# Strassen's form for slices 8 to 15 of the first MLP, and two kinds of sums moved into PSUM

## The chip, the cores and the metric

The kernel runs on one core of one Trainium2 chip. The metric is the device time of one execution in microseconds (us); lower is better.

## What is computed

A decayed linear attention (2 batches, 8 heads, 768 positions, 64 features a head) gives 1536 tokens of 512 features. Two MLPs follow, each with a hidden width of 2048:

```
h = x @ w_in                      # 1536x512 @ 512x2048
g = h * clip(h + 3, 0, 6) / 6     # second MLP: max(0.01 h, h)
x = g @ w_out                     # 1536x2048 @ 2048x512
```

The weights arrive as 64-bit floats and are turned into 32-bit ones on the chip.

## The kernel before, in words

**Tiles.** The tokens are three tiles t of 512. The hidden width is 16 slices f of 128. A step (l, t, f) is one slice of layer l for one token tile: `gemm1` (lines 465 to 477) makes the hidden block of 128 x 512 in one PSUM bank, an activation follows, and `gemm2` (508 to 525) adds the slice's share to four output banks acc0 to acc3, one for each quarter e of 128 output columns. Every operand is held as a high and a low part (`wh`, `wl`, `xh`, `xl`, `Gh`, `Gl`), and each product of two of them is three matmuls (high x high, high x low, low x high). So `gemm1` is 4 x 3 = 12 matmuls of 128x128 by 128x512, and `gemm2` is 12 as well, three for each e.

**Blocks.** The slices of layer 0 go in blocks of 1, 3, 4, 4, 4, those of layer 1 in four blocks of 4 (`BLOCKS`, line 30). In a block, all slices of a token tile add up in PSUM; then `collect` (527 to 535) adds the four banks to `SUM[t]` in SBUF, on VectorE (line 532), or copies them there in a layer's first block, on ScalarE (line 534). In layer 0, tile 1 uses two "a" banks in place of acc0 and acc1 (`acc_bank`, 505).

**Layer 0.** A step is: `gemm1` into an "h" bank; `gate_a` on ScalarE (line 482), `gate_b` on VectorE (486), `g_high` on ScalarE (492), `g_low` on VectorE (499); `gemm2`.

**Layer 1.** Token tiles 0 and 1 (`PAIR`) and two neighbouring slices form a 2 x 2 block product, which `product` (588 to 605) computes in Strassen's form (Winograd's variant): seven products of 6 matmuls each, four sums of weight halves (`w_sum`, `s_high`, `s_low`, 418 to 437) and four sums of input halves (T1 to T4: `x_sum`, `x_split`, 576 to 586). Products 0, 3, 5, 6 add up in one "h" bank, 1 and 4 in a second one, and 2 in an "a" bank. Between them, `keep` (607, ScalarE, line 610) copies the bank as it stands into an SBUF tile `ux`, and `join` (613, VectorE, line 614) adds a bank to such a copy: these are the blocks C11 (products 0 and 2), C12 and C22; the fourth block is the bank itself after product 6. Tile 2 goes by plain `gemm1` into "a" banks. Between the layers, VectorE and ScalarE split the new inputs and make T1 to T4 (lines 541 to 543 and 577 to 585).

**Weights.** Each half slice is loaded (line 371) and converted by two operations of ScalarE (378, 382) and four of VectorE (388 to 401), then split by one of each (409, 413). There are 6 buffers for a slice's weights ("w"), 4 for raw loads, 3 for conversions ("cv").

**Order.** Nothing is left to a scheduler at run time. `Order.issue` (58 to 112) plays the work through with the costs and buffers given in `add`, and always starts, on an idle engine, the ready operation that is due first; that order is each engine's program. Due times run back from the matmuls: 5.45 us a step in layer 0 (`T_STEP`), a written-out list per block in layer 1 (lines 650 to 665). Buffers are counted as `takes` and `frees`. The pools s, Gx and ux open once the attention is done (`open_late`, 561).

Of the kernel before, what the change touches and what calls it, by code (L numbers as in the profile page):

```python
# [23 lines left out]
P = 128  # L24
# [5 lines left out]
BLOCKS = ((1, 3, 4, 4, 4), (4, 4, 4, 4))  # L30

# [84 lines left out]
def decay_attention_two_mlps(ctx: ExitStack, tc: tile.TileContext, qkk, vv, lam, w1, w2, out):  # L116
# [24 lines left out]
    NS = len(steps)  # L141
    step_of = {}
# [275 lines left out]
    def w_sum(p, i):  # L418
        def fn(_):
            t1, t2, raw = (x.bitcast(F32) for x in (CV[1, 2 * p, 0][0], CV[1, 2 * p + 1, 0][0], RAW[1, 2 * p + 1, 0]))  # L420
# [4 lines left out]
            nc.vector.tensor_tensor(out=out[:, i], in0=a, in1=b, op=op)  # L425
            SB[p, "f"] = out
        return fn

    def s_high(p):
        def fn(_):  # L430
            SB[p] = new("s", [P, 2, 4, 2 * P], F32R)
            nc.scalar.copy(out=SB[p][:, 0], in_=SB[p, "f"])
        return fn

    def s_low(p):
        return lambda _: nc.vector.tensor_tensor(out=SB[p][:, 1], in0=SB[p, "f"], in1=SB[p][:, 0].bitcast(F32),
                                                 op=ALU.subtract)

    alloc_w, composed, low = {}, {}, {}
    for l in range(2):  # L440
        for f in range(NF):
            for j in range(2):
                h = (l, f, j)
                held = l == 1 and j == 0
# [9 lines left out]
            if l and f % 2:  # L454
                p, i = f // 2, None
                for n in range(4):
                    i = add(("dve", 0.43), w_sum(p, n), after=[composed[l, f - 1, 0], composed[l, f, 0], i])
                hi = add(("act", 1.05), s_high(p), after=[i], takes=["s"])
                s_ready[p] = add(("dve", 1.22), s_low(p), after=[hi], frees=["raw"])
                add(("none", 0.0), nothing, after=[i, low[l, f - 1, 0], low[l, f, 0]], frees=["cv"] * 2)  # L460
# [4 lines left out]
    def gemm1(s):  # L465
        def fn(_):
# [3 lines left out]
            ps = PH[s] = new("a" if l else "h", [P, TT], F32)  # L470
# [7 lines left out]

    def gate_a(s):
        def fn(_):  # L480
            U[s] = new("u", [P, TT], F32)
            nc.scalar.activation(out=U[s], in_=PH[s], func=AF.Relu, bias=three, scale=1.0)  # L482
        return fn

    def gate_b(s):
        return lambda _: nc.vector.scalar_tensor_tensor(out=U[s], in0=U[s], scalar=6.0, in1=PH[s], op0=ALU.min,  # L486
                                                        op1=ALU.mult)

    def g_high(s):
        def fn(_):  # L490
            G[s] = [new("G", [P, TT], F32R, n) for n in ("Gh", "Gl")]
# [13 lines left out]
    def acc_bank(s, e):  # L505
        return "a" if e < 2 and steps[s][2] % 2 and not steps[s][0] else f"acc{e}"

    def gemm2(s, e):
        def fn(_):
# [4 lines left out]
            if first:  # L514
# [7 lines left out]
            for n, (a, x) in enumerate(terms):  # L522
                nc.tensor.matmul(ACC[e], a, x, start=(first and n == 0), stop=(last and n == 2))  # L523
# [33 lines left out]
    XT, CS = {}, {}  # L557
# [71 lines left out]
    gates = {}  # L629

    def second(s, gl, w_frees):
# [4 lines left out]
        for e in range(4):  # L636
            bank = acc_bank(s, e)
            prev2 = add(("pe", 0.68), gemm2(s, e), due2[s], after=[gl, w_ready[l, f, 1], prev2],
                        takes=[bank] if first else [], frees=([] if e < 3 else w_frees))
            if not last:  # L640
                continue
            c = add(("dve", 0.69) if b else ("act", 0.58), collect(s, e), due2[s] + T_COLLECT,
                    after=[prev2, *taken.get((t, e), [])], frees=[bank])
            sums.append(c)
            taken[t, e] = [c]
# [3 lines left out]

    n0 = NS // 2  # L650
    at = T_FIRST + T_STEP * n0
    due_p = {}
    for b in range(len(BLOCKS[1])):
        fs = [f for f in range(starts[1][b], starts[1][b + 1])]
        one, two = (lambda i: ("1", fs[i])), (lambda t, i: ("2", b, t, fs[i]))
        before = [("2", b - 1, 2, fs[i] - 4) for i in (2, 3)] if b else []
        for item in [("S", fs[0] // 2), *before, ("S", fs[2] // 2), two(0, 0), two(0, 1), one(0), two(0, 2), two(0, 3),
                     one(1), two(1, 0), two(1, 1), one(2), two(1, 2), two(1, 3), one(3), two(2, 0), two(2, 1)]:
            due_p[item] = at
            at += 9.52 if item[0] == "S" else 2.72  # L660
    b = len(BLOCKS[1]) - 1
    due_p["2", b, 2, NF - 2], due_p["2", b, 2, NF - 1] = at, at + 2.72
    for s in range(n0, NS):
        l, b, t, f = steps[s]
        due1[s], due2[s] = due_p["1", f], due_p["2", b, t, f]

    for s in range(n0):
        l, b, t, f = steps[s]
        last = f + 1 == starts[l][b + 1]
        xs = [x_ready[c] for c in range(t * SPT, (t + 1) * SPT)]  # L670
        g1 = add(("pe", 2.73), gemm1(s), due1[s], after=[w_ready[l, f, 0], prev1] + xs, takes=["h", "G"])
        prev1 = g1
        ua = add(("act", 0.69), gate_a(s), after=[g1], takes=["u"])
        gb = add(("dve", 0.69), gate_b(s), after=[ua], frees=["h"])
        gh = add(("act", 0.63), g_high(s), after=[gb])
        gl = add(("dve", 0.69), g_low(s), after=[gh], frees=["u"])
        sums = second(s, gl, ["G"] + ["w"] * (t == NTT - 1))
        if last and b + 1 == len(BLOCKS[l]):
            sums_of[t], last1[t] = sums, g1
    add(("none", 0.0), open_late, after=att_ops, frees=[n for n in late for _ in range(late[n])])  # L680

    split = {}
    for e in (0, 2):
        hi = add(("act", 1.05), split_x(2, e, False), after=[last1[2]] + sums_of[2][e:e + 2])
        split[2, e] = add(("dve", 1.22), split_x(2, e, True), after=[hi])
        taken[2, e] = taken[2, e + 1] = [split[2, e]]
    x_op = {}

    def split_ops(n, after):
        hi = add(("act", 1.05), x_split(n, False), after=after)  # L690
        x_op[n] = add(("dve", 1.22), x_split(n, True), after=[hi])

    sa, sb = sums_of[PAIR[0]], sums_of[PAIR[1]]
    la, lb = last1[PAIR[0]], last1[PAIR[1]]
    split_ops("B11", [la, *sa[:2]])
    split_ops("B21", [la, *sa[2:]])
    split_ops("B22", [lb, *sb[2:]])
    t1 = add(("dve", 1.22), x_sum("T1", "B12", "B11"), after=[x_op["B11"], *sb[:2]])
    split_ops("T1", [t1])
    t3 = add(("dve", 1.22), x_sum("T3", "B22", "B12"), after=[t1, *sb[2:]])  # L700
    t2 = add(("dve", 1.22), x_sum("T2", "B22", "T1"), after=[t3, x_op["B22"]])
    split_ops("T2", [t2])
    split_ops("T3", [t3, lb])
    t4 = add(("dve", 1.22), x_sum("T4", "B21", "T2"), after=[t2, x_op["B21"]])
    split_ops("T4", [t4])
    for t, e, ops in ((0, 0, [x_op["T1"], t2]), (0, 2, [x_op["T4"]]), (1, 0, [x_op["T3"]]), (1, 2, [x_op["T2"], t4])):
        taken[PAIR[t], e] = taken[PAIR[t], e + 1] = ops

    gate = {}
    for p in range(NF // 2):  # L710
        f1, f2 = 2 * p, 2 * p + 1
        d = due_p["S", p]
        s_at = {(f, t): next(s for s in range(n0, NS) if steps[s][2:] == (t, f)) for f in (f1, f2) for t in PAIR}
        ops = []

        def prod(i, after=(), takes=()):
            an, bn = A_B[i]
            w = s_ready[p] if an[0] == "S" else w_ready[1, 2 * p + int(an[1]) - 1, 0]
            ops.append(add(("pe", 1.36), product(p, i), d + 1.36 * i, after=[w, x_op[bn], *ops[-1:], *after],
                           takes=list(takes)))  # L720
            return ops[-1]

        k1 = add(("act", 0.59), keep(p, 0), after=[prod(0, takes=["h"])], takes=["ux"])
# [71 lines left out]
```

## Time and profile before

| | us |
|---|---|
| three runs | 573.12, 575.12, 575.61 (median 575.12) |
| the profiled execution | 573.51 |
| its span, first to last instruction | 571.3 |
| mean granted TensorE clock in it | 0.995 |

In the profile, PE is TensorE, PEld its weight loads (they overlap matmuls), DVE VectorE, ACT ScalarE, POOL GpSimd. A name as `h<-xh,wh` is output and inputs; L475 is line 475. "Idle before" is the engine's idle time just before an instruction, with what ended it. A matmul's recorded duration (389 ns) includes its way through the array, and the next one starts before it ends: what one costs is the distance between starts.

### The profile page before, as it was taken

How to read it: one execution, taken by the hardware profiler on the slowest of the kernel's cores; microseconds unless marked ns; L12 is line 12 of the kernel's file. 1: busy time of each engine (PE TensorE's matmuls, PEld its weight loads, DVE VectorE, ACT ScalarE, POOL GpSimd, SP SyncE). 2: the span in 40 equal slices, each digit the busy share in tenths (PEclk: the TensorE clock that was granted, in tenths of full speed). 3: DMA queues.
4: the chain of work that ended last, by engine and by line, in shares of the span. 5: the costliest groups of instructions: out<-in, count | busy, mean ns of one | idle time of the engine just before them, and what ended most of it. 6: DMA issues, size and time to landing. Idle time of an engine off the chain costs nothing.

```text
span 571.3 us, 8498 instructions
## 1 busy us (share of the span) xinstructions
PE 557.7 (98%) x3396; PEld 462.1 (81%) x3396; DVE 414.0 (72%) x676; ACT 304.0 (53%) x510; POOL 28.3 (5%) x33
## 2 busy tenths in 40 slices
PE   8888999999999999999999999999999999999996
PEld 5877888888888888888888888888888888888885
DVE  8678889998848972698879898479864987653222
ACT  5687875557227532564536667477435653443110
POOL 6561000000000000000000000000000000000000
PEclk9899999999999999999999999999999999999999
DMA  8892333224303230012120114213221121000332
GB/s 332 325 357 99 111 110 111 97 87 149 110 1 108 77 110 1 17 57 74 75 74 1 37 38 141 81 38 111 73 75 37 38 74 38 0 1 1 75 73 73
DMA packets 14536, 49.81 MB, mean 87 GB/s; under 512 B 1698, under 2 KB 1698, under 8 KB 14498
## 3 DMA queue, kind: packets, MB, share of 16 engines
q1 hardware_dynamic: 14176, 48.77, 25.3%
q8 instruction: 26, 0.43, 0.3%
q10 hardware_dynamic: 322, 0.52, 0.3%
q14 instruction: 12, 0.10, 0.1%
HBM read 46.14 MB, written 3.15 MB: 86 GB/s over the span
## 4 chain that ended last, share of the span: by engine, by line
PE 91%; DVE 0%; issue 0%
PE acc L523 42%; PE h L475 23%; PE h L602 11%; PE a L475 8%; PE a L523 4%; PE a L602 2%; PE h L308 1%; PE a L296 1%; DVE sums L532 0%; PE pair L271 0%
## 5 line engine op out<-in xcount | busy, mean ns | idle before, releaser
L482 ACT ACTIVATE u<-h,three 128x512 f32<-128x512 f32 x48 | 33.1, 690 | 79.8 <-PE h L475 79.4
L475 PE MATMUL h<-xh,wh 128*128 128x512 f32 x192 | 74.9, 390 | 0.0
L475 PE MATMUL h<-xl,wh 128*128 128x512 f32 x192 | 74.7, 389 | 0.0
L475 PE MATMUL h<-xh,wl 128*128 128x512 f32 x192 | 74.7, 389 | 0.0
L532 DVE TENSOR_TENSOR sums<-acc,sums 128x512 f32<-128x512 f32 x76 | 50.7, 688 | 19.8 <-PE acc L523 19.8
L523 PE MATMUL acc<-Gh,wh 128*128 128x512 f32 x160 | 62.3, 390 | 0.0
L523 PE MATMUL acc<-Gh,wl 128*128 128x512 f32 x160 | 62.3, 389 | 0.0
L523 PE MATMUL acc<-Gl,wh 128*128 128x512 f32 x160 | 62.2, 389 | 0.0
L486 DVE SCALAR_TENSOR_TENSOR u<-u,h 128x512 f32<-128x512 f32 x48 | 32.9, 685 | 26.8 <-ACT u L482 26.7
L409 ACT CAST wh<-t 128x512 fp32r<-128x512 f32 x64 | 38.9, 618 | 24.2 <-DVE t L401 14.5
L523 PE MATMUL acc<-wh,Gh 128*128 128x512 f32 x128 | 49.8, 389 | 0.0
L523 PE MATMUL acc<-wl,Gh 128*128 128x512 f32 x128 | 49.8, 389 | 0.0
L523 PE MATMUL acc<-wh,Gl 128*128 128x512 f32 x128 | 49.8, 389 | 0.0
L401 DVE CUSTOM_DVE_ANT_0 t<-t,c 128x1024 uint16<-128x1024 uint16 x64 | 45.0, 703 | 2.2
L413 DVE TENSOR_TENSOR wl<-t,wh 128x512 fp32r<-128x512 f32 x64 | 42.9, 686 | 4.0 <-ACT wh L409 3.8
L399 DVE SCALAR_TENSOR_TENSOR t<-raw,t 128x512 uint32<-128x512 uint32 x64 | 44.7, 698 | 1.3
L378 ACT ACTIVATE c<-raw 128x512 uint32<-128x512 uint32 x64 | 42.6, 668 | 5.6 <-DVE t L401 4.6
L382 ACT ACTIVATE t<-raw 128x512 f32<-128x512 f32 x64 | 42.5, 664 | 5.0 <-DVE wl L413 5.0
L502 DVE TENSOR_TENSOR Gl<-u,Gh 128x512 fp32r<-128x512 f32 x24 | 16.6, 690 | 39.1 <-ACT Gh L619 39.0
L475 PEld LDWEIGHTS h<-xh,wh 128*128 128x128 f32 x192 | 36.0, 188 | 7.5
L475 PEld LDWEIGHTS h<-xl,wh 128*128 128x128 f32 x192 | 36.0, 188 | 7.5
L475 PEld LDWEIGHTS h<-xh,wl 128*128 128x128 f32 x192 | 36.0, 188 | 7.5
(128 smaller groups left out, 1120.6 us busy)
## 6 DMA issues: line engine op xcount, KB each, us to landing
raw<-w SPq DMA_DIRECT2D x64, 512.0 KB, 3.3
sums<-qkk SPq DMA_DIRECT2D x12, 768.0 KB, 6.8
vs<-vv SPq DMA_DIRECT2D x6, 512.0 KB, 5.4
out<-sums SPq DMA_DIRECT2D x20, 128.0 KB, 2.3
out<-sums ACTq DMA_DIRECT2D x4, 128.0 KB, 3.3
lam_sb<-lam ACTq DMA_DIRECT2D x1, 0.0 KB
```

Source lines behind the costliest of these rows:

```text
L378: nc.scalar.activation(out=CV[h][1], in_=RAW[h][:, :, 0], func=AF.Copy, scale=2.0 ** -29)
L382: return lambda _: nc.scalar.activation(out=CV[h][0].bitcast(F32), in_=RAW[h][:, :, 1].bitcast(F32), func=AF.Abs)
L399: nc.vector.scalar_tensor_tensor(out=t, in0=RAW[h][:, :, 1], scalar=0xC0000000, in1=t, op0=ALU.bitwise_and, op1=ALU.bitwise_or)
L401: nc.vector.tensor_tensor(out=t, in0=t, in1=c, op=ALU.add)
L409: nc.scalar.copy(out=cut(*h, 0), in_=CV[h][0].bitcast(F32))
L413: return lambda e: eng[e].tensor_tensor(out=cut(*h, 1), in0=CV[h][0].bitcast(F32), in1=cut(*h, 0).bitcast(F32), op=ALU.subtract)
L475: nc.tensor.matmul(ps, a[:, 0, ws], x[:, k, :], start=(n == 0), stop=(n == 3 * KC - 1))
L482: nc.scalar.activation(out=U[s], in_=PH[s], func=AF.Relu, bias=three, scale=1.0)
L486: return lambda _: nc.vector.scalar_tensor_tensor(out=U[s], in0=U[s], scalar=6.0, in1=PH[s], op0=ALU.min, op1=ALU.mult)
L523: nc.tensor.matmul(ACC[e], a, x, start=(first and n == 0), stop=(last and n == 2))
L532: nc.vector.tensor_tensor(out=acc, in0=ps, in1=acc, op=ALU.add)
L602: nc.tensor.matmul(ps, ws[a][:, k * P:(k + 1) * P], xs[b][:, k], start=(i < 3 and n == 0), stop=(n == 5), skip_group_check=True)
```

## The change

1. **Layer 0, slices 8 to 15** (blocks 3 and 4, `SINGLE = 3`): tiles 0 and 1 go by `product` as in layer 1, tile 2 by plain `gemm1` into "a" banks. The weight sums are made for these slices too. The input halves exist there only as high and low parts, so VectorE first adds the parts of four halves (`x_whole`), makes T1 to T4 by four differences (`x_diff`), and splits them (`x_split`, high on ScalarE, low on VectorE). The whole values lie in the two "s" buffers until they are split.
2. **C11 in PSUM**, in both layers: `keep` of product 0 copies the "h" bank into an "a" bank, and product 2 adds to it there, with no `join`; products 0 and 1 still start banks of their own.
3. **Half of the sums over blocks, in PSUM**: in blocks 3 and 4 of layer 0, for e = 0 and 2, `seed` copies `SUM[t]` into the bank on ScalarE before the first `gemm2`, and `collect` is a copy back on ScalarE. For e = 1 and 3 VectorE adds as before. Tile 1 uses acc0 and acc1 there.
4. The due times of these blocks are written out as layer 1's; in block 4, tiles 0 and 1 come first and tile 2's `gemm1` between their end and its own `gemm2`.

```diff
+SINGLE = 3
+    paired = lambda l, f: l == 1 or f >= starts[0][SINGLE]
...
-            if l and f % 2:
+            if paired(l, f) and f % 2:
...
-            ps = PH[s] = new("a" if l else "h", [P, TT], F32)
+            ps = PH[s] = new("a" if paired(l, f) else "h", [P, TT], F32)
...
+    seeded = lambda s, e: steps[s][0] == 0 and steps[s][1] >= SINGLE and e % 2 == 0
+    def seed(s, e):
+        def fn(_):
+            n = acc_bank(s, e)
+            ps = PA["seed", s, e] = pool["acc"].tile([P, TT], F32, tag=n, name=n)
+            nc.scalar.copy(out=ps, in_=SUM[steps[s][2]][:, e, :])
+        return fn
...
-            if b:
+            if b and not seeded(s, e):
                 nc.vector.tensor_tensor(out=acc, in0=ps, in1=acc, op=ALU.add)
             else:
                 nc.scalar.copy(out=acc, in_=ps)
...
+    def x_whole(n):
+        t, e = {"B11": (0, 0), "B21": (0, 2), "B12": (1, 0), "B22": (1, 2)}[n]
+        def fn(g):
+            if n in ("B11", "B22"):
+                SPARE[n == "B22"] = pool["s"].tile([P, 2, 2, TT], F32, tag="s", name="x_spare")
+            xh, xl = (x[:, e:e + 2].bitcast(F32) for x in X[PAIR[t]])
+            eng[g].tensor_tensor(out=spare(n), in0=xh, in1=xl, op=ALU.add)
+        return fn
+    def x_diff(n, a, b):
+        return lambda e: eng[e].tensor_tensor(out=spare(n), in0=spare(a), in1=spare(b), op=ALU.subtract)
...
-                    nc.tensor.matmul(ps, ws[a][:, k * P:(k + 1) * P], xs[b][:, k], start=(i < 3 and n == 0),
+                    nc.tensor.matmul(ps, ws[a][:, k * P:(k + 1) * P], xs[b][:, k], start=(i < 2 and n == 0),
...
+    def keep(l, p, i):
+        def fn(_):
+            if i:
+                CS[l, p, i] = new("ux", [P, TT], F32)
+            else:
+                CS[l, p, i] = PA["S", l, p, 1] = new("a", [P, TT], F32)
+            nc.scalar.copy(out=CS[l, p, i], in_=PA["S", l, p, BANK[i]])
+        return fn
...
+            if first and in_seed:
+                start = add(("act", 0.6), seed(s, e), after=[*taken[t, e], bank_last[bank]], takes=[bank])
...
+        if end:
+            line = [*(two(t, i) for t in PAIR for i in range(4)), one(0), one(1), two(2, 0), one(2), two(2, 1), one(3),
+                    two(2, 2), two(2, 3)]
+        else:
+            line = [two(0, 0), two(0, 1), one(0), two(0, 2), two(0, 3), one(1), two(1, 0), two(1, 1), one(2),
+                    two(1, 2), two(1, 3), one(3), two(2, 0), two(2, 1)]
+        for item in [pair(0), *rest, pair(2), *line]:
...
+        k1 = add(("act", 0.59), keep(l, p, 0), after=[prod(0, takes=["h"])], takes=["a"])
+        k5 = add(("act", 0.59), keep(l, p, 1), after=[prod(1, takes=["h"])], takes=["ux"])
+        c11 = prod(2, [k1])
...
+            if l == 0:
+                ua = add(("act", 0.69), gate_a(s), after=[c], takes=["u"])
+                gb = add(("dve", 0.69), gate_b(s), after=[ua], frees=[bank or "ux"])
+                gh = add(("act", 0.63), g_high(s, n), after=[gb], takes=[n])
...
+    for n, after in (("T1", [t2]), ("T2", [t4]), ("T4", [t4]), ("T3", [t3, last1[0, PAIR[1]]])):
+        hi = add(("act", 1.05), x_split(n, False, spare), after=after)
+        x_op[0, n] = [add(halves, x_split(n, True, spare), after=[hi])]
```

## Rows read from the trace of the kernel before

**Rows 1.** The page: span, and each engine's busy time, share, instructions.
```profile
span 571.3 us, 8498 instructions
PE 557.7 (98%) x3396; PEld 462.1 (81%) x3396; DVE 414.0 (72%) x676; ACT 304.0 (53%) x510; POOL 28.3 (5%) x33
```

**Rows 2.** What TensorE waited for: total, times, longest.
```profile
PE pair L271 <- issue: 2.9, 2, 2.2
PE a L296 <- issue: 2.8, 1, 2.8
PE a L296 <- POOL kd L261: 1.1, 1, 1.1
```

**Rows 3.** Busy time by stretch: layer 0's blocks, then two blocks of layer 1.
```profile
49.00:114.30 65.30, 65.30 (x427) 54.22 (x424) 57.99 (x101) 47.15 (x83) 0.00 (x0) 1.00 0.31 103
114.30:179.60 65.30, 65.30 (x289) 54.05 (x288) 50.78 (x89) 32.67 (x55) 0.00 (x0) 1.00 0.25 84
179.60:244.90 65.30, 65.30 (x290) 54.06 (x289) 44.70 (x78) 29.24 (x49) 0.00 (x0) 1.00 0.20 65
244.90:310.20 65.30, 65.30 (x290) 54.07 (x289) 55.52 (x88) 34.31 (x51) 0.00 (x0) 1.00 0.17 57
372.50:435.10 62.60, 62.60 (x278) 51.84 (x277) 44.72 (x77) 35.32 (x61) 0.00 (x0) 1.00 0.20 68
```

**Rows 4.** The chain that ended last, around a pair of layer 1: start, us.
```profile
387.40 1.36 PE h L602 x6
388.76 0.68 PE acc L523 x3
389.44 1.36 PE h L602 x6
390.80 1.36 PE a L602 x6
...
404.40 2.72 PE a L475 x12
```

**Rows 5.** VectorE's groups, shapes apart: count, busy us, mean ns, idle before.
```profile
L532 DVE TENSOR_TENSOR sums<-acc,sums 128x512 f32<-128x512 f32 x76 | 50.7, 688 | 19.8 <-PE acc L523 19.8
L486 DVE SCALAR_TENSOR_TENSOR u<-u,h 128x512 f32<-128x512 f32 x48 | 32.9, 685 | 26.8 <-ACT u L482 26.7
L614 DVE TENSOR_TENSOR ux<-h,ux 128x512 f32<-128x512 f32 x16 | 11.0, 690 | 9.0 <-PE h L602 9.0
L436 DVE TENSOR_TENSOR s<-raw,s 128x1024 fp32r<-128x1024 f32 x8 | 9.8, 1219 | 0.1
L425 DVE TENSOR_TENSOR raw<-t 128x256 f32<-128x256 f32 x16 | 6.7, 420 | 0.2
L577 DVE TENSOR_TENSOR sums<-sums 128x1024 f32<-128x1024 f32 x4 | 4.9, 1220 | 0.0
```

**Rows 6.** VectorE's busy time (fourth figure) around the start of block 3.
```profile
145.00:155.00 10.00, 10.00 (x46) 8.28 (x45) 8.82 (x17) 4.27 (x7) 0.00 (x0) 1.00 0.40 138
155.00:165.00 10.00, 10.00 (x46) 8.29 (x45) 2.62 (x4) 2.01 (x3) 0.00 (x0) 1.00 0.05 21
165.00:179.60 14.60, 14.60 (x66) 12.08 (x65) 11.21 (x21) 8.57 (x15) 0.00 (x0) 1.00 0.11 36
179.60:190.00 10.40, 10.40 (x47) 8.63 (x46) 9.31 (x18) 7.01 (x12) 0.00 (x0) 1.00 0.34 109
```

**Rows 7.** ScalarE's groups, shapes apart: count, busy us, mean ns, idle before.
```profile
L482 ACT ACTIVATE u<-h,three 128x512 f32<-128x512 f32 x48 | 33.1, 690 | 79.8 <-PE h L475 79.4
L610 ACT COPY ux<-h 128x512 f32<-128x512 f32 x24 | 14.1, 588 | 17.8 <-PE h L602 17.8
L534 ACT COPY sums<-acc 128x512 f32<-128x512 f32 x22 | 12.7, 589 | 0.8
L432 ACT CAST s<-raw 128x1024 fp32r<-128x1024 f32 x8 | 8.4, 1050 | 2.4 <-DVE raw L425 2.4
```

**Rows 8.** ScalarE in order of time: the copy after product 0, and a cast.
```profile
388.80 0.59 ACT L610 COPY ux<-h 128x512 f32<-128x512 f32 x1 [0.19 <-PE h L602]
...
391.32 1.05 ACT L432 CAST s<-raw 128x1024 fp32r<-128x1024 f32 x1
```

More of the change, by code (lines that the diff above doesn't have):

```diff
@@ L513, in fn @@
             first, last = f == starts[l][b], f + 1 == starts[l][b + 1]
-            if first:
+            if first and seeded(s, e):
+                ACC[e] = PA["seed", s, e]
+            elif first:
                 n = acc_bank(s, e)
@@ L522, in fn @@
             for n, (a, x) in enumerate(terms):
-                nc.tensor.matmul(ACC[e], a, x, start=(first and n == 0), stop=(last and n == 2))
+                nc.tensor.matmul(ACC[e], a, x, start=(first and n == 0 and not seeded(s, e)), stop=(last and n == 2),
+                                 skip_group_check=seeded(s, e))
             PA["acc", s, e] = ACC[e]
@@ L629, in decay_attention_two_mlps @@
     gates = {}
+    bank_last = {}
     def second(s, gl, w_frees):
@@ L648, in second @@
         return sums
[L650 to L658, printed above, removed]
+    n1, n0 = starts[0][SINGLE] * NTT, NS // 2
@@ new lines, in decay_attention_two_mlps @@
+    at = T_FIRST + T_STEP * n1
+    due_p, rest = {}, []
+    for l, b in [(0, b) for b in range(SINGLE, len(BLOCKS[0]))] + [(1, b) for b in range(len(BLOCKS[1]))]:
+        fs, end = range(starts[l][b], starts[l][b + 1]), l == 0 and b + 1 == len(BLOCKS[0])
+        pair, one, two = (lambda i: ("S", l, fs[i])), (lambda i: ("1", l, fs[i])), (lambda t, i: ("2", l, t, fs[i]))
+        if end:
[5 more added lines that the diff above has]
+        for item in [pair(0), *rest, pair(2), *line]:
@@ L668, in decay_attention_two_mlps, with one @@
+    last_s, gate = {}, {}
+    def one(s, after):
+        nonlocal prev1
         l, b, t, f = steps[s]
[L669 to L710, printed above, removed]
+        h = "a" if paired(l, f) else "h"
@@ L711, in decay_attention_two_mlps, with pair @@
+        gate[s] = add(("dve", 0.69), g_low(s), after=[gh], frees=["u"]), "G"
+    def pair(l, p):
         f1, f2 = 2 * p, 2 * p + 1
-        d = due_p["S", p]
-        s_at = {(f, t): next(s for s in range(n0, NS) if steps[s][2:] == (t, f)) for f in (f1, f2) for t in PAIR}
+        d = due_p["S", l, f1]
         ops = []
@@ L752, in decay_attention_two_mlps @@
-    for s in range(n0, NS):
-        gl, n = gate[s]
-        second(s, gl, [n] + ["w"] * (steps[s][2] == NTT - 1))
+        k1 = add(("act", 0.59), keep(l, p, 0), after=[prod(0, takes=["h"])], takes=["a"])
+        k5 = add(("act", 0.59), keep(l, p, 1), after=[prod(1, takes=["h"])], takes=["ux"])
+        c11 = prod(2, [k1])
+        k2 = add(("act", 0.59), keep(l, p, 3), after=[prod(3, [k1])], takes=["ux"])
+        c12 = add(("dve", 0.69), join(l, p, 3, 2), after=[prod(4, [k5]), k2], frees=["h"])
@@ new lines, in pair, with seconds @@
+        add(("none", 0.0), nothing, after=ops, frees=["s"])
+    def seconds(l, b):
+        for s in range(NS):
+            if steps[s][:2] == (l, b):
+                sums = second(s, gate[s][0], [gate[s][1]] + ["w"] * (steps[s][2] == NTT - 1))
+                if sums and b + 1 == len(BLOCKS[l]):
+                    sums_of[l, steps[s][2]] = sums
+    x_of = lambda t: [x_ready[c] for c in range(t * SPT, (t + 1) * SPT)]
+    for b in range(SINGLE):
+        for s in range(n1):
+            if steps[s][1] == b:
+                one(s, x_of(steps[s][2]))
+        seconds(0, b)
@@ new lines, in decay_attention_two_mlps @@
+    op_late = add(("none", 0.0), open_late, after=att_ops, frees=[n for n in late for _ in range(late[n])])
+    x_op, halves = {}, ("dve", 1.22)
+    for n, t in (("B11", 0), ("B21", 0), ("B22", 1)):
+        x_op[0, n] = x_of(PAIR[t])
+    w11, w12, w22, w21 = (add(halves, x_whole(n), after=[op_late, *x_of(PAIR[t])], takes=["s"] * (n in ("B11", "B22")))
+                          for n, t in (("B11", 0), ("B12", 1), ("B22", 1), ("B21", 0)))
+    t1 = add(halves, x_diff("T1", "B12", "B11"), after=[w11, w12])
@@ new lines, in block @@
+    def block(l, b):
+        fs = range(starts[l][b], starts[l][b + 1])
+        for f in fs[::2]:
+            pair(l, f // 2)
+        for f in fs:
+            one(at_step[l, 2, f], x_of(2) if l == 0 else [split[2, 0], split[2, 2]])
+        seconds(l, b)
+    for b in range(SINGLE, len(BLOCKS[0])):
+        block(0, b)
+    split = {}
+    for e in (0, 2):
+        hi = add(("act", 1.05), split_x(2, e, False), after=[last1[0, 2]] + sums_of[0, 2][e:e + 2])
+        split[2, e] = add(("dve", 1.22), split_x(2, e, True), after=[hi])
+        taken[2, e] = taken[2, e + 1] = [split[2, e]]
```

176 lines of the change are left out of this document (103 added, 73 removed).

## The prediction

> **What bounds the kernel now.** I read the page's busy times first [rows 1]: TensorE is busy for 557.7 of 571.3 us, VectorE for 72% and ScalarE for 53%. A busy TensorE need not be a full one, so next came its waits [rows 2]: all of any size are in the attention's lines, ahead of 49 us, and none belongs to an MLP. The stretches by block say the same [rows 3]: from 49 us on TensorE is busy for 65.3 of every 65.3 us in layer 0, at a granted clock of 1.00 (2.4 GHz). The chain that ended last gives the price of one matmul [rows 4]: 6 take 1.36 us and 12 take 2.72 us, start to start, so 0.2267 us each. The MLPs are therefore a gapless row of matmuls from 49 us to the last one, and their time is a count times 0.2267 us, as long as no wait opens.
>
> **TensorE, what goes.** For a pair of slices, tiles 0 and 1 now take 4 steps of 12 matmuls, 48 in all. In the changed form they take 7 products of 6, 42. Slices 8 to 15 are 4 pairs: 4 x 6 = 24 matmuls fewer, 24 x 0.2267 = 5.44 us. Nothing is added on TensorE: `gemm2` keeps its 12 matmuls, tile 2 its 12, and copying into a bank costs no matmul. A block of 4 slices goes from 288 matmuls (65.3 us) to 276 (62.6 us). Layer 1 shows such a block already, without a wait: 62.6 of 62.6 us busy [rows 3].
>
> The Trainium skill ("TensorE: Matmul & The Clock Gate", section "Back-to-back issue gap") gives about 131 ns a matmul in a stream with 512 columns. By it the sum would be an estimated 24 x 0.131 = 3.1 us; the rows of this case show 226.7 ns, and I take these.
>
> **VectorE, what comes.** Per new pair: four weight sums at 0.420, one low part at 1.219, two joins at 0.690, in all 4.28 us, 17.1 for four pairs. For the inputs: four whole values, four differences and four low parts, 12 operations of 128x1024, for which the nearest row is T1 to T4's between the layers at 1.220: 14.6 us. What goes: of layer 0's `collect`, 2 blocks x 3 tiles x 2 quarters = 12 at 0.688, 8.3 us; in layer 1 eight joins for C11, 5.5 us [rows 5]. The activations keep their number. In layer 0 that makes 17.1 + 14.6 - 8.3 = 23.4 us more. The joins gone from layer 1 I cost at nothing: TensorE has no wait there that they could end.
>
> Is there room? T1 to T4 and the sums of the first two pairs are due around 180 to 190 us: 14.6 + 2 x 2.9 = 20.4 us. From 49 to 179.6 us VectorE idles for 65.3 - 57.99 = 7.3 and 65.3 - 50.78 = 14.5, in all 21.8 us [rows 3]. The largest hole lies right ahead of the date: in 155 to 165 us it works for 2.62 of 10 us, since all buffers for weights are full [rows 6]. The conversion of a slice's second half is not needed until its `gemm2`, some 20 us after the first products, and can slide. So I cost the input sums at nothing; their cover is that hole, and if it fails they cost up to what they take. After that, block 3 has 44.7 us of work now, and would have 44.7 + 2 x 4.28 - 4.1 = 49.2 of 62.6; block 4 has the transition's sums in 55.5 now, and would have 60 of 62.6, but the new order ends tile 1 eight `gemm`s (21.8 us) ahead of layer 1, so its 12 us of sums lie there with few gates beside them.
>
> **ScalarE.** 12 more `keep` copies at 0.588, four casts for S and four for T at 1.050, 12 seeds and 12 copies out at 0.589 [rows 7]: 7.1 + 8.4 + 14.1 = 29.6 us. In blocks 2 to 4 it is busy for 29 to 35 of 65.3 us [rows 3], so this is hidden in sum. A seed writes PSUM from SBUF, a form that the rows don't hold at this size; I take the copy out, 0.589, and the gates from SBUF at 0.690.
>
> **The new waits.** Product 2 now waits for the copy of product 0; behind it stand, in TensorE's program, products 3 to 6. The copy starts 0.04 us after the sixth matmul's 1.36 us are over (388.80 against 387.40 + 1.36) and takes 0.59 [rows 4, 8]: done at 389.39, and with product 1 directly behind, product 2 would start at 387.40 + 2.72 = 390.12. That leaves 0.73 us. If a cast of 1.05 had just started on ScalarE [rows 8], the copy would end at 390.44, and TensorE would wait 0.32 us. Bounds for 12 pairs: 0 and 3.9 us. I take 0, for the planner knows this wait and has other work to put in between, as the 0.68 us of `gemm2` in rows 4.
>
> A seed needs the last tile's copy out and then its own copy, 1.2 us, ahead of the next tile's first `gemm2` of that quarter. Three quarters lie in between, 3 x 0.68 = 2.04 us [rows 4]; one ScalarE operation of 0.69 [rows 7] in front still fits. In most changes of tile a `gemm1` of 2.72 us or a pair lies between as well; only from tile 0 to 1 in block 4 there is none. Bounds: 0 and 0.7 us; I take 0.
>
> Held longer: an "a" bank from the copy to C11's gate (two banks, and tile 2's `gemm1`s come in another part of the block); `u` from a gate until a `Gx` is free (three, of which at most two wait so); one of four raw buffers for layer 0's pairs, so that a load leaves SP's queue later, with DMA at 0.20 to 0.25 busy [rows 3]. Each can shift work by an operation's length, and there is other work to fill with. No DMA is added, and POOL has no work after the attention.
>
> **The sum.** 573.51 - 5.44 = 568.1 us for the profiled execution. That one lies 1.6 us below the median of the three runs; from the median it is 575.12 - 5.44 = 569.7 us, the number I name. Likeliest range: 573.12 - 5.44 - 1 = 566.7 (the attention's waits, 6.8 us in rows 2, may shrink by a little as the order shifts) to 572.2.
>
> **The rivals.** A measurement of this kernel can tell 0.5%, 2.9 us, from no change.
>
> *Handed back in small waits.* The 3.9 us of the copies and 0.7 of the seeds are paid: 569.7 + 4.6 = 574.3. For it: ScalarE's program is in order, and each pair now has a step of 1.36 us with 0.73 us of slack, twelve times. Against it: layer 1's handoffs have the same look now and cost nothing [rows 3].
>
> *VectorE becomes the bound (slower).* The place is from the start of block 3 to its second pair, and the same place in block 4. If the holes ahead of 114 us can't be used, 20.4 - 14.5 = 5.9 us of input sums are left when product 1 wants T1. Then in two pairs and the `gemm2`s between them (2 x 9.52 + 5.44 = 24.5 us) VectorE would have 8 gates of 1.38, four joins, four `collect`s and four half conversions of 2.94: 11.0 + 2.8 + 2.8 + 11.8 = 28.4, so 3.9 short, twice: 569.7 + 5.9 + 7.8 = 583.4. It decides the sign once the waits pass 5.44 us, and makes the kernel measurably slower past 8.3. For it: VectorE at 89% from 49 to 114 us. Against it: the hole of 7.4 us at 155 us [rows 6], and work that can slide.
>
> *A cheaper matmul.* If the 24 matmuls lay beside others in the array and cost 3.1 us: 572.0. This is the rule cited above, as a mechanism; every count in rows 4 speaks against it.
>
> **How the numbers follow.** Forecast 0.68; small waits 0.19; VectorE 0.11; the cheaper matmul 0.02. Faster by over 0.5% are the first and the last: 0.70; within 0.5% the second, 0.19; slower the third, 0.11. Range 566.5 to 576.0: it holds the forecast, the cheaper matmul and the small waits with 1.7 us for the spread of runs, and leaves VectorE's case out.
>
> **What would show it.** Right: TensorE with 3372 instructions; no MLP line among its waits; the two blocks at 62.6 us, clock 1.00; VectorE near 432 us in sum, its hole at 155 us filled. Small waits would show as idle time of TensorE ahead of the products' line, ended by ScalarE's copy. VectorE's case would show as idle time at 170 to 200 us ended by VectorE, with its busy share at 95% or more. The forecast is wrong if these waits add up to over 2.5 us, or if the stretch ahead of 49 us grows.

## The result

The changed kernel takes 566.94 us (median of 5 runs, 565.72 to 570.67) against 573.55 us before (median of 5, 572.21 to 575.61): a ratio of 0.989, 95% interval 0.9858 to 0.9922. Forecast were 5.44 us less; the medians give 6.6 less, and the interval reaches from 4.5 to 8.1. Taken again beside the experiments, the kernel before had medians of 572.81 us (15 runs) and 572.60 (7); against these the changed kernel's median is 5.9 and 5.7 less.

The traces allow a sharper measure. From the start of the first `gemm1` matmul to the start of the last matmul I call the **MLP stretch**. It leaves out the last stores and all of the attention but its last 160 matmuls, which stand within the stretch's first 12 us in both kernels. Before the change it is one stretch of 516.84 us without a gap, after it one of 511.50 (busy time by stretch; the columns are those of [rows 3]). The kernel before, and below it the last part of its attention:

```profile
49.01:565.85 516.84, 516.84 (x2420) 428.09 (x2416) 374.04 (x624) 270.88 (x453) 0.00 (x0) 1.00 0.20 65
...
40.00:49.00 9.00, 6.20 (x194) 5.79 (x188) 8.62 (x10) 6.24 (x11) 4.63 (x4) 1.00 0.62 224
```

The changed kernel, and below it VectorE's old hole [rows 6], the entry into layer 1, and the last part of the attention:

```profile
51.55:563.05 511.50, 511.50 (x2396) 423.59 (x2392) 389.28 (x644) 295.96 (x497) 0.00 (x0) 1.00 0.21 65
...
155.00:165.00 10.00, 10.00 (x46) 8.29 (x45) 8.86 (x14) 6.79 (x10) 0.00 (x0) 1.00 0.34 107
...
315.00:330.00 15.00, 15.00 (x67) 12.30 (x66) 14.00 (x24) 13.47 (x23) 0.00 (x0) 1.00 0.30 105
...
40.00:49.00 9.00, 7.36 (x181) 7.04 (x182) 6.37 (x8) 4.42 (x8) 2.77 (x3) 0.81 0.78 297
```

TensorE is busy in all of both stretches: 2420 records became 2396, 24 fewer, and 5.34 us went, 0.2225 us each. The attention is another matter. In this one profiled execution (570.67 us, the slowest of the five) the clock granted from 40 to 49 us was 0.81 (the lower level, 1.2 GHz, from 42.3 to 45.7 us; in the 6.3 us before that TensorE was busy for 3.10), against 1.00 before, and the first `gemm1` came at 51.55 us instead of 49.01. Over the 14 traces of this study that start lies between 46.6 and 51.6 us, the kernel before in between. So a single time can't tell 2 us. A stretch can: traces of kernels with the same count and no wait in the MLPs agree within 0.2 us (table below), though each kernel was traced only once. The experiments below are judged by the stretch.

The page of the changed kernel, which answers to [rows 1]:

```profile
span 568.5 us, 8504 instructions
PE 554.9 (98%) x3372; PEld 460.3 (81%) x3372; DVE 430.0 (76%) x696; ACT 329.1 (58%) x554; POOL 28.2 (5%) x33
```

Its longest waits of TensorE, which answer to [rows 2]:

```profile
PE pair L274 <- issue: 5.5, 2, 3.2
PE a L299 <- POOL kd L264: 1.1, 1, 1.1
```

TensorE has 3372 instructions as forecast, and no line of an MLP among its waits. VectorE rose by 16 us (18 forecast), ScalarE by 25 (29.6 forecast; its 44 new operations are there, 554 against 510).

### The profile page after: what moved, and what is told of

Read it like the earlier page. It is cut to its first block, busy times and chain, and to the rows that moved or that the text cites. A ratio compares the mean times of both kernels' runs of the same rounds, so it can differ in the third digit from the quotient of the medians.

```text
span 568.5 us, 8504 instructions
## 1 busy us (share of the span) xinstructions
PE 554.9 (98%) x3372; PEld 460.3 (81%) x3372; DVE 430.0 (76%) x696; ACT 329.1 (58%) x554; POOL 28.2 (5%) x33
## 4 chain that ended last, share of the span: by engine, by line
PE 96%; issue 1%; DMA 1%; POOL 1%; DVE 0%; SPq 0%; POOLq 0%
PE acc L540 44%; PE h L638 17%; PE h L478 12%; PE a L478 11%; PE a L638 3%; PE pair L274 2%; PE a L299 2%; PE h L311 2%; PE a L540 2%; DMA vs<-vv 1%; DVE sums L550 0%; POOL kd L264 0%; PE h L179 0%; POOL vs L260 0%; SPq L243 0%
## 5 line engine op out<-in xcount | busy, mean ns | idle before, releaser
L540 PE MATMUL acc<-Gh,wl 128*128 128x512 f32 x144 | 56.0, 389 | 0.0
L540 PE MATMUL acc<-Gl,wh 128*128 128x512 f32 x144 | 56.0, 389 | 0.0
L664 ACT ACTIVATE u<-a 128x512 f32<-128x512 f32 x24 | 14.4, 599 | 59.4 <-PE a L478 57.6
L416 DVE TENSOR_TENSOR wl<-t,wh 128x512 fp32r<-128x512 f32 x64 | 43.0, 686 | 7.4 <-ACT wh L412 7.3
L402 DVE SCALAR_TENSOR_TENSOR t<-raw,t 128x512 uint32<-128x512 uint32 x64 | 44.1, 689 | 1.3
L487 ACT ACTIVATE u<-h,three 128x512 f32<-128x512 f32 x28 | 19.3, 689 | 40.6 <-PE h L478 36.9
L478 PE MATMUL h<-xh,wh 128*128 128x512 f32 x96 | 37.6, 391 | 0.0
L478 PE MATMUL h<-xh,wl 128*128 128x512 f32 x96 | 37.4, 389 | 0.0
L478 PE MATMUL h<-xl,wh 128*128 128x512 f32 x96 | 37.4, 389 | 0.0
L478 PE MATMUL a<-xh,wh 128*128 128x512 f32 x96 | 37.3, 389 | 0.0
L478 PE MATMUL a<-xl,wh 128*128 128x512 f32 x96 | 37.3, 389 | 0.0
L478 PE MATMUL a<-xh,wl 128*128 128x512 f32 x96 | 37.3, 389 | 0.0
```

The costliest lines, as they stand in the source:

```text
L402: nc.vector.scalar_tensor_tensor(out=t, in0=RAW[h][:, :, 1], scalar=0xC0000000, in1=t, op0=ALU.bitwise_and, op1=ALU.bitwise_or)
L416: return lambda e: eng[e].tensor_tensor(out=cut(*h, 1), in0=CV[h][0].bitcast(F32), in1=cut(*h, 0).bitcast(F32), op=ALU.subtract)
L478: nc.tensor.matmul(ps, a[:, 0, ws], x[:, k, :], start=(n == 0), stop=(n == 3 * KC - 1))
L487: nc.scalar.activation(out=U[s], in_=at_src(s), func=AF.Relu, bias=three, scale=1.0)
L540: nc.tensor.matmul(ACC[e], a, x, start=(first and n == 0 and not seeded(s, e)), stop=(last and n == 2), skip_group_check=seeded(s, e))
```

## The experiments

All stretches in one table. "Count" is 516.84 us less 0.2267 for each matmul saved.

| kernel | matmuls saved | count | MLP stretch |
|---|---|---|---|
| before | 0 | 516.84 | 516.84 |
| the change | 24 | 511.40 | 511.50 |
| C11 in PSUM alone (layer 1) | 0 | 516.84 | 516.91 |
| Strassen's form for block 4 alone | 12 | 514.12 | 514.19 |
| without parts 2 and 3 | 24 | 511.40 | 515.53 |
| without part 3 (seeds) | 24 | 511.40 | 511.40 |
| without part 2 (C11) | 24 | 511.40 | 511.59 |
| whole values three times | 24 | 511.40 | 512.92 |
| whole values five times | 24 | 511.40 | 524.17 |
| first copy six times | 24 | 511.40 | 533.16 |
| slices 4 to 15 | 36 | 508.68 | 519.96 |
| slices 4 to 15, all quarters seeded | 36 | 508.68 | 519.27 |
| no parts 2 and 3, low parts on GpSimd | 24 | 511.40 | 526.04 |
| slices 4 to 15, sums on GpSimd | 36 | 508.68 | 540.42 |

### One part alone, and one block alone

C11 in PSUM, nothing else (layer 0 as before; the input sums are cut out):

```diff
-SINGLE = 3
+SINGLE = 5
...
-    x_op, halves = {}, ("dve", 1.22)
...
+    x_op = {}
```

> Only the second part: C11 added in PSUM in layer 1; layer 0 as before, no input sums, no seeds. Measured by the MLP stretch, from the start of the first gemm1 matmul to the start of the last matmul: 516.84 us before, 511.50 with the whole change. Theory (the MLPs are a gapless row of matmuls; VectorE's 5.5 us of joins in layer 1 lay beside it): 516.8, within 0.3. Rival, the copies are waited for: 8 pairs at up to 0.32 us, up to 519.4, with idle time of TensorE ahead of the product line ended by ScalarE. Rival, the joins were in the way somewhere: below 516.3.

Measured 516.91: neither a gain nor a loss that one trace can tell. Eight joins (5.5 us of VectorE) gone from layer 1 are worth nothing by themselves, and eight products that now wait for a copy cost nothing.

Block 4 alone:

```diff
-SINGLE = 3
+SINGLE = 4
```

> The whole change for block 4 alone, slices 12 to 15 (SINGLE = 4): 2 pairs, 12 matmuls fewer than before. Theory (count times 0.2267 us): MLP stretch 516.84 - 2.72 = 514.1, within 0.3. Rival (a fixed loss at the entry into the paired blocks, as the 0.1 us that the whole change lacks, or more): 514.2 to 514.8; rival (the saving comes from the order, not the count): 512 or 516.

Measured 514.19. Half the matmuls give half the gain; there is no fixed loss at the entry. With the whole change this makes three points on one line: 0, 12 and 24 matmuls at 516.84, 514.19 and 511.50.

### Strassen's form without the two reliefs

The first part alone: `join` for C11 again, all sums over blocks on VectorE.

```diff
-    seeded = lambda s, e: steps[s][0] == 0 and steps[s][1] >= SINGLE and e % 2 == 0
+    seeded = lambda s, e: False
...
-        k1 = add(("act", 0.59), keep(l, p, 0), after=[prod(0, takes=["h"])], takes=["a"])
+        k1 = add(("act", 0.59), keep(l, p, 0), after=[prod(0, takes=["h"])], takes=["ux"])
...
-        c11 = prod(2, [k1])
+        c11 = add(("dve", 0.69), join(l, p, 0, 1), after=[prod(2, takes=["a"]), k1], frees=["a"])
```

> Only the first part: Strassen's form for slices 8 to 15, C11 by a join on VectorE in both layers, all sums over blocks on VectorE, no seeds. VectorE has 8.3 us of collects and 2.8 of joins more in layer 0 than with the whole change, 5.5 more in layer 1. Theory (VectorE has room: with the whole change it idles for 24 us between 114 and 305 us): MLP stretch 511.5, within 0.5, the same time as the whole change. Rival (parts 2 and 3 are what makes room): waits of TensorE for VectorE in layer 0's blocks 3 and 4, up to 11.1 us, a stretch of 513 to 522.

My theory fell here. The stretch is 515.53, 1.3 us less than before in place of 5.3, and the time 571.75 us (ratio 0.998, interval 0.9959 to 1.0002), which is no gain that the times can tell. The place was the surprise. All of TensorE's waits in the MLPs are these three (line, what it waited for: us in total, times, longest):

```profile
PE acc L540 <- DVE wl L416: 1.2, 1, 1.2
PE acc L540 <- ACT wh L412: 1.2, 1, 1.2
PE h L638 <- DVE ux L650: 0.9, 1, 0.9
```

The stretches of the same run:

```profile
242.00:305.00 63.00, 63.00 (x280) 52.16 (x279) 55.46 (x88) 38.02 (x59) 0.00 (x0) 1.00 0.15 51
...
315.00:330.00 15.00, 11.73 (x50) 8.84 (x49) 14.14 (x24) 10.81 (x19) 0.00 (x0) 1.00 0.39 140
```

They lie between 315 and 330 us, at the entry into layer 1, and not in blocks 3 and 4. The chain that ended last shows what TensorE waited for. From 317.6 to 327.0 us it runs through VectorE with hardly a break (start, us; the first lines of that part):

```profile
313.49 4.09 PE h L638 x18
317.59 0.03 issue
317.61 0.02 DVEq L650
317.63 0.04 issue
317.68 0.69 DVE ux L650
318.37 0.60 DVE Gl L507
318.97 1.21 DVE wl L416 x2
320.17 1.14 DVE xl L559
```

There VectorE must do everything at once: layer 1's input sums, the conversion of its first weights (whose buffers come free only as layer 0's last steps end), their sums, the joins of its first pair. My reading: what was put off in layer 0 is paid here.

The new theory: what counts is VectorE's backlog up to this point. The two reliefs together take 8.3 + 2.8 + 1.4 = 12.5 us of VectorE away ahead of it (the 1.4 are the joins of layer 1's first two pairs); 4.0 of these were missing; so the whole change has some 8.5 us of room. Each relief was then taken out by itself, with the corresponding lines of the diff above:

> The whole change without part 3: no seeds, the 12 sums over blocks go back to VectorE (8.3 us), C11 stays in PSUM. The run without both parts lost 4.0 us of MLP stretch (515.53 against 511.50), all of it between 317 and 327 us, at the entry into layer 1, where the chain runs through VectorE. Theory now (VectorE carries a backlog there; both parts together take 8.3 + 2.8 + 1.4 = 12.5 us from it up to that point, 4.0 of which were missing, so some 8.5 us of room are left with the whole change): 8.3 fits just so, 511.5 to 511.9. Rival (the seeds are what counts): about 515. Rival (what lies in the paired blocks counts, not the sum up to layer 1): 512 to 513 with waits at 184 to 305 us.

> The whole change without part 2: C11 by a join on VectorE in both layers (2.8 us in layer 0, 1.4 in the first two pairs of layer 1), seeds stay. Backlog theory: 4.2 of some 8.5 us of room, MLP stretch 511.5, within 0.3. Rival (the joins are what counts, since they stand in the first pairs of layer 1, where the run without both parts waited): 513 to 515, waits at 310 to 330 us ended by the join.

Measured 511.40 and 511.59, with no wait in the MLPs in either. Neither relief is needed alone; without both, three quarters of the gain are lost. What lies in the paired blocks is not the point, for the seeds' 8.3 us all lie there.

### More load on VectorE

To test the room from the other side, each whole value (high plus low part) was computed again, three or five times in all, into the same place, and the planner was told:

```diff
+    def whole_sums(n, t):
+        op = add(halves, x_whole(n), after=[op_late, *x_of(PAIR[t])], takes=["s"] * (n in ("B11", "B22")))
+        for _ in range(2):
+            op = add(halves, x_whole(n, True), after=[op])
+        return op
```

> The whole change with each of the four whole values (high plus low part) computed three times: 8 more VectorE operations of 1.22 us, 9.8 us, due before block 3, known to the planner. Backlog theory (what counts is VectorE's load in sum up to layer 1's first block; some 8.5 us of room, from the run without parts 2 and 3): about 1.3 us of waits, at 315 to 330 us, MLP stretch 511.5 to 513. Rival (the hole ahead of block 3 is the cover, as the prediction had it: VectorE idles for 5.2 + 6.2 us from 49 to 180 us): 9.8 fits, 511.5, no waits. Rival (this place has no room at all): waits at 170 to 200 us, up to 521.

> The same five times: 16 more operations, 19.5 us (tile 2's gemm1 in layer 0's paired blocks also waits until the pairs' gates of tile 0 are done). Backlog theory: 19.5 - 8.5 = 11 us of waits, stretch about 522.5, part of them now ahead of layer 1. Hole theory: 19.5 - 11.4 = 8 us, all at 170 to 200 us, stretch 519.5. If loads slide further than either says: below 518.

Three times: 512.92, and the one wait in the MLPs is again at the entry into layer 1, 165 us behind the last of the extra sums (they start between 65 and 158.5 us):

```profile
323.67 0.39 PE L540 MATMUL acc<-wh,Gl 128*128 128x512 f32 x1
325.21 0.50 PE L638 MATMUL h<-xh,wh 128*128 128x512 f32 x1 [1.15 <-ACT Gh L658]
325.55 0.39 PE L638 MATMUL h<-xl,wh 128*128 128x512 f32 x1
```

The hole ahead of block 3 is not the cover: by its size 9.8 us would have fitted into it. It was hardly used. From 49 to 179.6 us VectorE idles for 11.4 us in the change and still for 10.5 with the extra sums, so some 8.9 of their 9.8 us only pushed other work behind 180 us. The changed kernel, then this run:

```profile
49.00:114.30 65.30, 65.30 (x492) 54.47 (x489) 60.10 (x102) 48.62 (x86) 2.27 (x2) 1.00 0.29 97
114.30:179.60 65.30, 65.30 (x290) 54.09 (x289) 59.13 (x94) 32.37 (x50) 0.00 (x0) 1.00 0.19 59
...
49.00:114.30 65.30, 65.30 (x458) 54.27 (x455) 60.22 (x103) 47.40 (x84) 1.13 (x1) 1.00 0.29 97
114.30:179.60 65.30, 65.30 (x290) 54.07 (x289) 59.92 (x86) 28.49 (x45) 0.00 (x0) 1.00 0.13 44
```

In the wait's lines above, ScalarE is named as the one that ended the wait; its `leak` before it stood behind a conversion that had waited for VectorE.

The three lines of this wait also show what a wait costs. Idle time counts from the recorded end, 0.39 us after a start, where the next matmul would have come after 0.23: that is 0.16. And the matmul after the wait comes 0.34 ahead of its successor in place of 0.23: 0.11. So 1.15 + 0.27 = 1.42 us, just what the stretch lost against 511.50. For the three waits above it makes 3.3 + 0.8 = 4.1, against 4.0 lost.

Five times: 524.17. Now VectorE can't catch up and the waits begin at block 3. (This run also makes tile 2's `gemm1`s wait for the gates of tile 0, so its point holds more than the added sums.)

```profile
180.00:200.00 20.00, 16.70 (x70) 12.53 (x68) 19.13 (x30) 13.22 (x20) 0.00 (x0) 1.00 0.15 53
200.00:242.00 42.00, 36.13 (x155) 28.56 (x155) 39.55 (x72) 27.68 (x48) 0.00 (x0) 1.00 0.29 100
```

Put in order of the load added ahead of layer 1's first block, the runs lie close to one bent line:

| VectorE, us more than with the change | 0 | 4.2 | 8.3 | 9.8 | 12.5 | 19.5 |
|---|---|---|---|---|---|---|
| MLP stretch, us more | 0 | 0.09 | -0.10 | 1.42 | 4.03 | 12.67 |

Up to 8.3 nothing happens; 9.8 and 12.5 lose what goes beyond some 8.4; only the last lies above (11.1 by this line), with its waits elsewhere. The 8.4 is read off from these points, two of which lie beyond the bend with the waits at this place. It is far less than VectorE's idle time: in the changed kernel that is 29 us from 49 to 305 us, of which 11.4 lie ahead of block 3.

### The copy that product 2 waits for

The copy of product 0 into the "a" bank, six times in place of once, unknown to the planner:

```diff
-            nc.scalar.copy(out=CS[l, p, i], in_=PA["S", l, p, BANK[i]])
+            for _ in range(1 if i else 6):
+                nc.scalar.copy(out=CS[l, p, i], in_=PA["S", l, p, BANK[i]])
```

> The whole change with the copy of product 0 into the second bank done six times in place of once, unknown to the planner: ScalarE's copy ends some 2.4 us later in all 12 pairs. With the whole change the copy ends 1.27 us ahead of product 2 in seven pairs, 1.95 and 2.29 in two, 3.05 to 4.67 in three. Theory (product 2 waits for the copy once this slack is used, and nothing of it is won back): 7 x 1.2 + 0.5 + 0.2 = about 9 us, stretch 520 to 522, idle time of TensorE ahead of product 2 ended by ScalarE. Rival (other work takes it up): under 515. Rival (ScalarE's delay upsets the gates too): over 525.

In the change itself the handoff looks like this, in a pair of layer 1 (in order of time: the last matmul of product 0, the copy, the first of product 1, the first of product 2):

```profile
370.61 0.39 PE L638 MATMUL h<-xh,wl 128*128 128x512 f32 x1
...
371.03 0.57 ACT L649 COPY a<-h 128x512 f32<-128x512 f32 x1 [1.43 <-PE h L638]
...
371.51 0.39 PE L638 MATMUL h<-T1h,s 128*128 128x512 f32 x1
...
372.88 0.39 PE L638 MATMUL a<-xh,wh 128*128 128x512 f32 x1
```

The copy ends at 371.60, product 2 starts at 372.88: 1.27 us to spare, since 0.68 us of `gemm2` lie between products 0 and 1. The tightest seven pairs all have 1.27, the others more; none waits.

With six copies the stretch is 533.16: 21.7 us more, where I expected 9. The six start 0.60 us apart, not some 0.48 as other copies do: each starts only after the recorded end of the one before, whose bank it writes again (3.58 us in all); so they end 3.0 us later, and the same sum gives 14.0. The trace lists 13.0 us in nine waits for the copy, 1.6 for other copies behind it and 2.0 for a gate; with 0.27 for each of these 12 waits it makes 19.8 of the 21.7. The handoff does bind once its slack is used, and the delay spreads further than the waits for the copy alone.

### Twelve slices, and GpSimd

Strassen's form for block 2 as well (with two more dependencies, so that the planner does not run out of buffers):

```diff
-SINGLE = 3
+SINGLE = 2
...
+        first = [s_ready[l, p], *x_op[0, "T1"], *x_op[0, "T2"], *x_op[0, "T3"], *x_op[0, "T4"]] if l == 0 else []
```

> The whole change for one block more, slices 4 to 15 (SINGLE = 2). A pair's first product also waits until its weight sums and all of T1 to T4 are there, and tile 2's gemm1 until the pairs' gates of tile 0 are done. 12 matmuls fewer than the whole change. If VectorE had room here too: 511.5 - 2.7 = 508.8. My theory says it has not: the input sums are due some 65 us earlier, near 114 us, and up to there VectorE idles for only 5.2 us of 65.3, against 14.6 us of input sums and 5.8 of weight sums; some 10 to 15 us of waits at the start of block 2, a stretch of 518 to 524, slower than the kernel before.

Measured 519.96, and 576.21 us (ratio 1.0072, interval 1.0044 to 1.0099): 0.7% slower than before the change, with 36 matmuls fewer. VectorE is the bound at the start of block 2:

```profile
49.00:114.30 65.30, 65.30 (x425) 54.19 (x424) 61.17 (x96) 44.43 (x75) 0.00 (x0) 1.00 0.18 65
114.30:140.00 25.70, 20.21 (x86) 15.55 (x85) 24.16 (x43) 16.97 (x29) 0.00 (x0) 1.00 0.31 102
```

Seeding all four quarters there:

```diff
-    seeded = lambda s, e: steps[s][0] == 0 and steps[s][1] >= SINGLE and e % 2 == 0
+    seeded = lambda s, e: steps[s][0] == 0 and steps[s][1] >= SINGLE
```

> Slices 4 to 15 in Strassen's form as in the run before (519.96), with all four quarters seeded in place of two: 18 more sums over blocks (12.4 us) leave VectorE for ScalarE, in blocks 2 to 4. Backlog theory: the waits of that run were VectorE's, at the start of block 2 and at the entry into layer 1; the first stay, the others go: 512 to 517. If all of them go: 508.8, the fastest version. Rival (ScalarE, with 36 copies more, becomes the bound): over 520.

519.27: almost nothing. I had put part of the first run's waits at the entry into layer 1; the trace has all of them between 129 and 164 us, and the first copy back that replaces a sum of VectorE's is at 161 us.

GpSimd is idle after the attention. In the next run it takes low parts of weights (on the kernel without parts 2 and 3):

```diff
-                low[h] = w_ready[h] = add(("dve", 0.7), w_low(h), after=[hi], frees=[] if held else ["cv"])
+                low[h] = w_ready[h] = add([("dve", 0.7), ("pool", 1.2)], w_low(h), after=[hi], frees=[] if held else ["cv"])
```

> The run without parts 2 and 3, with the low parts of the weights (51 of 64, 128x512, SBUF to SBUF) on GpSimd instead of VectorE, at a planned 1.2 us each (nearest row: 1.146 for 64x512 there). VectorE gets rid of 51 x 0.69 = 35 us. If VectorE's load is the cause of the 4.0 us, and GpSimd works beside it: MLP stretch 511.5, all waits at 317 to 327 us gone. Rival (GpSimd takes longer than planned, or holds VectorE up): GpSimd's mean over 1.5 us or VectorE's operations of two SBUF inputs over 0.69, waits of TensorE ended by GpSimd, 516 and more.

526.04, 10.5 us worse than without GpSimd. The waits at the entry into layer 1 are gone, as they should be if VectorE's load causes them; but TensorE now waits early: 6.8 of the 7.8 us listed in the MLP stretch lie between 64 and 136 us. Groups of this run, shapes apart (columns as in [rows 5]):

```profile
L416 POOL TENSOR_TENSOR wl<-t,wh 128x512 fp32r<-128x512 f32 x52 | 73.5, 1413 | 391.3 <-ACT wh L412 375.7 <-DVE Gl L504 5.6 <-DVE sums L550 3.7
L416 DVE TENSOR_TENSOR wl<-t,wh 128x512 fp32r<-128x512 f32 x12 | 10.5, 877 | 7.4 <-ACT wh L412 7.3
L402 DVE SCALAR_TENSOR_TENSOR t<-raw,t 128x512 uint32<-128x512 uint32 x64 | 50.8, 794 | 1.4
L491 DVE SCALAR_TENSOR_TENSOR u<-u,h 128x512 f32<-128x512 f32 x28 | 19.1, 683 | 7.4 <-ACT u L487 7.1
```

The same groups of the changed kernel:

```profile
L416 DVE TENSOR_TENSOR wl<-t,wh 128x512 fp32r<-128x512 f32 x64 | 43.0, 686 | 7.4 <-ACT wh L412 7.3
L402 DVE SCALAR_TENSOR_TENSOR t<-raw,t 128x512 uint32<-128x512 uint32 x64 | 44.1, 689 | 1.3
L491 DVE SCALAR_TENSOR_TENSOR u<-u,h 128x512 f32<-128x512 f32 x28 | 19.2, 687 | 10.8 <-ACT u L487 10.6
```

One low part costs GpSimd 1.41 us, where 1.2 were planned, and some of VectorE's operations with two operands in SBUF get longer. The mean goes from 0.69 to 0.79 for L402 and from 0.69 to 0.88 for its remaining low parts; it is a few that are hit (of L402 the median stays at 0.69, the longest takes 1.77). The two conversions with a single operand, in SBUF (L391, L394), go from 0.42 to 0.48 and from 0.43 to 0.49. Those that read PSUM (L491) stay at 0.68 to 0.69. So 52 operations less (36 us at 0.69) left VectorE as busy as it was. This run's page, then that of the run without GpSimd:

```profile
PE 557.6 (96%) x3372; PEld 456.0 (79%) x3372; DVE 444.5 (77%) x668; ACT 317.6 (55%) x530; POOL 101.0 (17%) x85
...
PE 552.9 (97%) x3372; PEld 456.9 (80%) x3372; DVE 446.3 (78%) x720; ACT 317.2 (56%) x530; POOL 27.9 (5%) x33
```

The Trainium skill ("SBUF — State Buffer", section "Who interferes with whom") says that VectorE and GpSimd share a pair of SBUF ports under an exclusive lock, and that a VectorE instruction with two SBUF inputs contends with a GpSimd instruction that reads SBUF. The rows of L402 and L416 agree.

How much of the 10.5 us is that, and how much the planner's wrong cost, was not tried. A part is the clock: behind two waits (TensorE busy for 3.92 us from 105.0 to 110.7) the granted clock was 0.50, the lower level, from 110.7 to 114.1 us, and its eight matmuls came 0.43 us apart in place of 0.23 (8 x 0.20, an estimate of 1.6 us).

The input sums on GpSimd, for slices 4 to 15, and low parts of weights there as in the run before:

```diff
-    x_op, halves = {}, ("dve", 1.22)
+    x_op, halves = {}, [("pool", 2.3)]
```

> The run with slices 4 to 15 in Strassen's form, with its 12 operations of 128x1024 for the input sums on GpSimd (planned 2.3 us each) and the low parts of the weights there whenever VectorE is busy. With VectorE it had a stretch of 519.96, 11.2 us above its count of matmuls (508.8). If GpSimd is a free engine: 509 to 512, the fastest version. Rival (GpSimd's chain of sums is longer and in order, low parts of the weights stand behind it): 515 to 525.

540.42, and 596.30 us (ratio 1.04, interval 1.0361 to 1.0439), the slowest of all, well beyond what either theory said. The trace shows how it begins. TensorE's largest waits, 8.1 and 4.1 us, end at 82.5 and 87.4 us, long before the sums are due. Beside GpSimd's sums, most of VectorE's conversions take 2.2 to 2.8 us each in place of 0.42 to 0.69, about one to each operation of GpSimd; the gate L491 behind them, which reads PSUM, takes its usual 0.68 us, but starts late, and TensorE's wait of 8.1 us is for `Gh`, which ScalarE makes from it. GpSimd and VectorE in order of time, and the granted clock of the same stretch, at the lower level (in the 6.1 us before it TensorE was busy for 2.38):

```profile
72.88 5.57 POOL L622 TENSOR_TENSOR x_spare<-x_spare 128x1024 f32<-128x1024 f32 x2
73.52 2.74 DVE L404 CUSTOM_DVE_ANT_0 t<-t,c 128x1024 uint16<-128x1024 uint16 x1
76.18 2.56 DVE L391 TENSOR_SCALAR t<-t 128x512 f32<-128x512 f32 x1
78.41 2.52 POOL L618 TENSOR_TENSOR x_spare<-xh,xl 128x1024 f32<-128x1024 f32 x1
78.77 2.45 DVE L394 TENSOR_SCALAR t<-t 128x512 uint32<-128x512 uint32 x1
81.14 0.68 DVE L491 SCALAR_TENSOR_TENSOR u<-u,h 128x512 f32<-128x512 f32 x1
...
78.10:91.70 13.60, 5.11 (x11) 3.73 (x12) 12.20 (x12) 5.42 (x10) 8.01 (x4) 0.50 0.13 40
```

The shares of the sums, the low parts and the clock in the whole loss were not told apart. No version here is shorter than the changed kernel by more than 0.1 us of stretch.

## Why the prediction was right, and where not

- **The gain.** 24 matmuls at 0.2267 us: 5.44 forecast, 5.34 measured in the stretch, and the runs with 0, 12 and 24 matmuls saved lie on one line. The estimate by the Trainium skill's 131 ns ("TensorE: Matmul & The Clock Gate", section "Back-to-back issue gap"), 3.1 us, does not hold here: each matmul gone is worth 0.22 us.
- **The 569.7.** The median came out at 566.94, 2.8 us lower and only 0.4 above the lower end of my range. Some 1.6 of these are the base: the median of before is 573.55 by five runs, and I had 575.12 by three; from 573.55 the same sum gives 568.1. The rest, 1.2 us, is within the scatter of the runs (565.72 to 570.67), of which one was traced, so its place stays open. That the time lay inside the range in spite of the base is partly luck.
- **The new waits.** Bounded by 0 and 3.9 us for the copies and 0.7 for the seeds, taken at 0, and 0 it was. The slack I gave for a product 2 directly behind product 1, 0.73 us, was taken from the chain's view, whose start is 0.16 us behind the matmul's own, so it is nearer 0.6; but the planner's order leaves at least 1.27 in every pair.
- **VectorE's cover.** Here the result was right and the reason wrong. I named the hole at 155 us and said that the input sums, if it failed, would cost up to what they take. The hole is filled (2.62 to 8.86 of 10 us), but only one of the twelve input operations starts in it: ten start between 66.9 and 153.9 us, and the rest of what was added to the hole is mostly conversion and sums of weights. By the runs above, the limit is the sum of VectorE's work up to layer 1's first block, with some 8.4 us left. And where I called block 4's end safe, because layer 1's sums get 21.8 us of their own, is the very place where the lack shows.
- **The reliefs.** I entered part 3's 8.3 us in VectorE's sum and priced part 2's joins in layer 1 at nothing. Either can go; with both gone, 4.0 of the 5.3 us go too. A term that costs nothing by itself can still be the cover of another.
- **The rival VectorE** had the mechanism but not the place. It is real at the start of a paired block only with more load: with slices 4 to 15, and with the sums five times.

## What to carry to other kernels

Where one engine's row of work is gapless, time is its count, and a saving lands in full as long as every other engine still keeps up; so ask not how busy the helper is on average but how much work it must have done by the next dense point, and test that by adding dummy work until it shows. Work that is put off is paid at the first place where nothing more can be put off, which here was 165 us later. Measure small changes by a stretch of the trace between two fixed instructions when the executions scatter by more than the change.

## What was not expected of the hardware

- A wait of TensorE costs 0.27 us more than its listed idle time: 0.16 because the record of the matmul before it ends late, and 0.11 because the next matmul is 0.34 us ahead of its successor in place of 0.23.
- The clock granted at the end of the attention was 0.81 in one profiled execution and 1.00 in another, and the start of the MLPs moved by 5 us over 14 traces. Where two kernels have the same count and no waits, their traces differ ahead of the MLPs and hardly within them.
- GpSimd takes 1.41 us for a 128x512 subtraction, SBUF to SBUF, and 2.6 to 2.7 us for a 128x1024 sum, and beside it VectorE's operations on SBUF alone get longer: by 14 to 28% in the mean of the groups named above, and mostly to 2.2 to 2.8 us in place of 0.42 to 0.69 beside those sums. Work moved to an idle GpSimd is not free for VectorE.
